# Chunked mLSTM state kept as row pairs of 64-row tiles instead of three-head blocks

## The chip, the cores and the metric

The kernel runs on one core of one Trainium2 chip. The metric is the device time of one execution in microseconds (us); the median of three runs stands for the kernel. One more execution was recorded by the hardware profiler, and all rows below come from it.

A core has five engines that work in parallel, each on its own queue in order: PE (TensorE, matrix products; its weight loads are listed apart as PEld), DVE (VectorE), ACT (ScalarE), POOL (GpSimd) and SP (SyncE, which here issues the DMAs). They wait for each other through semaphores. PE writes to PSUM, eight banks of 128 partitions by 512 float32 numbers; the other data lie in SBUF.

## The reference

Three layers follow one another. The change is in the first, a gated linear attention (mLSTM), over batch B = 2, heads H = 8, sequence S = 768, head size D = 40:

```python
for t in range(S):
    m_new = np.maximum(f_gate[:, :, t] + m, i_gate[:, :, t])
    f_stab = np.exp(f_gate[:, :, t] + m - m_new)
    i_stab = np.exp(i_gate[:, :, t] - m_new)
    m = m_new
    C = f_stab[:, :, None, None] * C + i_stab[:, :, None, None] * np.einsum('bhd,bhe->bhde', vt, kt)
    n = f_stab[:, :, None] * n + i_stab[:, :, None] * kt
    h_tilde = np.einsum('bhde,bhe->bhd', C, qt)
    nq = np.einsum('bhd,bhd->bh', n, qt)[:, :, None]
    y[:, :, t] = sigmoid(o_gate) * h_tilde / np.maximum(np.abs(nq), 1.0)
```

Behind it come a gated MLP with a mixing product along the sequence (`w_in`, `w_sp`, `w_out`) and a channel mix with squared ReLU (`w_k`, `w_v`, `w_r`). They are not touched.

## The kernel before

The sequence is cut into six chunks of 128 tokens; with two batches that makes twelve work items i, taken in the order `SEQ` (L44): chunk 0 of both batches, then chunk 1 of both, and so on. The item i - 1, on whose state item i rests, is therefore two positions earlier. Within a chunk the recurrence becomes matrix products:

- `scores` (L444) multiplies queries and keys of the chunk (tiles sc), `logd` (L474) makes the decay between two tokens (ld, then dt), `intra` (L570) multiplies the weighted scores with the values (av). The queries and keys of heads 0 to 3 lie on partitions 0 to 39, those of heads 4 to 7 on 64 to 103, so a product of 40 rows takes the upper or the lower half of PE's array; the matmuls of heads g and 4 + g alternate and write to two banks.
- `state` (L514) multiplies the keys, weighted by POOL in `key_weights` (kw, L503), with the values: what the chunk adds to the state (sp). Three heads stand together (`GRP`, L56): a product of 128 tokens by 120 rows by 123 columns holds nine 40 by 41 blocks, of which the three on the diagonal are wanted. ACT fades the old state with three activations (`fade`, L533, from `dec`), and DVE takes the wanted blocks out of PSUM with three operations under a block mask (`gather`, L541). The state is cn.
- `inter` (L552) reads the state with a second copy of the queries, laid out by groups of three heads, that comes with the keys and values in one load (kvq, `load_kv`, L331): three matmuls per item (ip), and one DVE operation that scales the result by a gate (nn).
- `normalise` (L583) adds both parts, `turn` (L615) transposes the result (tp, then xg).

In float32 each of these matmuls stands in the trace as two pairs of a weight load and a matmul record.

The order on each engine is made by a planner while the program is built. A position p of the pipeline holds tasks (`task`, L894): S0 (scores of the next item), I (`inter`), T (`state`), N0 and N1 (the two halves of `intra`), X (`turn`). The planner keeps its own clock with costs written in the code (`beat`, `chain`), takes the first of four tasks whose inputs it thinks ready, and fills in between with matmuls of the MLP's input product (`vpart`, `upart`: tiles vp and up), so many per task as `FILL` (L890) says. Where none is ready it issues junk matmuls (`heat`, tile wp). The elementwise work of a task is a chain of steps on DVE, ACT and POOL. PSUM tiles of this part come from a ring of six banks (`bank`, tag "at"): a matmul that starts a new tile waits until the tile six banks earlier has been read.

While this runs, weights of 64-bit words are turned into pairs of float32r tiles by `widen` (L252), in steps on ACT, DVE and POOL (tiles wbits, wsq, and w_v, w_u at the end).

The lines that the change touches are these:

Of the kernel before, what the change touches and what calls it, by code (L numbers as in the profile page):

```python
# [17 lines left out]
def tile_mlstm_gmlp_channelmix(  # L18
# [26 lines left out]
    P = 128  # L45
# [10 lines left out]
    GRP = ((0, 3), (3, 3), (6, 2))  # L56
# [239 lines left out]
    def rows3(t, w):  # L296
# [10 lines left out]
                            for nm, n in (("f2", P), ("i2", P), ("ex_sb", 120), ("pk_sb", 6 * NCH)))  # L307
    bm_sb = at.tile([120, 3], F32, name="bm_sb")
    mg = gp.tile([16, S + 1], F32, name="mg")
    ones = gp.tile([96, P], F32, name="ones")  # L310
    dec = at.tile([120, 6, NCH], F32, name="dec")
# [11 lines left out]
    def load_qk(i):  # L323
        b, c = divmod(i, NCH)
        t = at.tile([P, 2, 4, P], F32, tag="qk", name=f"qk{i}", bufs=2)
        for hh in range(2):
            e = load(t[64 * hh:64 * hh + D], qk[b, c, hh], 164)
        st["q", i], st["k", i] = t[:, 0], t[:, 1]
        st["at", i] = e

    def load_kv(i):  # L331
        b, c = divmod(i, NCH)
        n = H * D + H * DA + (3 * P if c > 0 else 0)
        t = at.tile([P, H * D + H * DA + 3 * P], F32, tag="kvq", name=f"kvq{i}", bufs=2)
# [3 lines left out]
        if c > 0:  # L338
            st["qc", i] = t[:120, H * (D + DA):].rearrange("p (g t) -> p g t", g=3)
# [174 lines left out]
    def state(i):  # L514
        b, c = divmod(i, NCH)
        vt = st["vt", i]
        if c == NCH - 1:
            return
        wait(("kw", i))
        kw = st.pop(("kw", i))  # L520
        sp = bank(psa, "at", f"sp{i}", ("Cs", i))
        if c == 0:
            st["C", b] = at.tile([120, H * DA], F32, name=f"cn{b}")
        cn = st["C", b]
# [6 lines left out]
        s3, c3 = (t.rearrange("p (h d) -> p h d", h=H) for t in (sp[:, :H * DA], cn))  # L531

        def fade():  # L533
            if i == SEQ[0]:
                act.copy(bm_sb, bm_raw)
            if c > 0:
                for g, (h0, n) in enumerate(GRP):
                    sl = slice(h0 * DA, (h0 + n) * DA)
# [7 lines left out]
        if c == 0:  # L546
            pool.memset(cn, 0.0)
        else:
            finish(("dec", 0), stall=False)
        chain(("C", i), ("A", 0.75 if c else 0.2, fade), ("V", 1.0, gather, ("Cs", i)))  # L550

    def inter(i):  # L552
        b, c = divmod(i, NCH)
        if c == 0:
            return
        wait(("C", i - 1))
        qt, cs = st.pop(("qc", i)), st["C", b]
        ip = bank(psa, "at", f"ip{i}", ("nn", i))
        for g, (h0, n) in enumerate(GRP):
# [5 lines left out]
        chain(("nn", i), ("V", 0.41, lambda: vec.tensor_tensor(  # L565
            out=nn, in0=ip[:, :H * DA].rearrange("p (h d) -> p h d", h=H), op=ALU.mult,
            in1=egate(b, c, 0).unsqueeze(2).to_broadcast([P, H, DA]))))
# [272 lines left out]
    bm_raw = at.tile([120, 3], F32, name="bm_raw")  # L840
    m2 = gp.tile([96, 2, P], F32, name="m2")
    lpk = gp.tile([96, 6 * NCH], F32, name="lpk")
# [8 lines left out]
    for a in 'k0 v0 q6 k6 v1 b v2 n'.split():  # L851
        dict(k=lambda: load_kv(SEQ[a != "k0"]), q=lambda: load_qk(SEQ[1]), n=lambda: load_qk(SEQ[2]),
             v=lambda: w_in_load("v", 1, int(a[1])), b=lambda: load(bm_raw, blockmask[:, 0:3 * DA:DA], 2))[a[0]]()
    w_in_split("v", hv)
    chain(("G0", 1), ("V", 0.26, lambda: scan(1, 2)), *[("V", 0.28, f) for f in late_steps], ready=6.9)
# [21 lines left out]
    for t, x in ((ex_sb, expand), (pk_sb, pick)):  # L877
        load(t, x, 48)
# [4 lines left out]
    def decays():  # L883
        dps = bank(psa, "at", "dps", ("dec", 0))
        pe.matmul(dps[:120, :6 * NCH], ex_sb, lpk, start=True, stop=True)
        beat(0.15)
        chain(("dec", 0), ("A", 0.1, lambda: act.activation(out=dec.rearrange("p j c -> p (j c)"),
                                                            in_=dps[:120, :6 * NCH], func=AF.Exp)))

    FILL = (6, 4, 1, 3, 1, 1, 1, 4)  # L890
# [6 lines left out]
    def position(p):  # L897
# [22 lines left out]
        def st_():  # L920
# [5 lines left out]
            state(i)  # L926
# [413 lines left out]
```

## Time and profile before

| | before |
|---|---|
| median of 3 runs | 307.42 us (307.24 to 307.59) |
| profiled execution | 307.6 us, span 305.9 us from the first to the last instruction |
| attention with its fillers | from about 8 us to 129 us of the span |
| PE busy / PEld busy | 296.7 us (97%) / 281.0 us (92%) |
| DVE / ACT / POOL busy | 225.0 us / 165.7 us / 143.7 us |
| granted TensorE clock | 1.000 of full speed (2.4 GHz) |

The busy time of PE overlaps itself, since matmuls are pipelined and their ends are modelled: how fast PE goes is read from the distance between starts, or from the pieces of the chain of waits, which do not overlap.

### The profile page before, as it was taken

The numbers are of one execution on the slowest core, as the hardware profiler recorded it, in microseconds if no ns is written. First come the engines' busy times: TensorE is split into PE (matmuls) and PEld (weight loads), VectorE is DVE, ScalarE is ACT, GpSimd is POOL, SyncE is SP. The second block draws the span as 40 slices with busy tenths as digits, with TensorE's granted clock in tenths as the row PEclk, the third lists the DMA queues.
The fourth block names the chain that finished last, engine by engine and source line by source line (L and its number), as shares of the span: only waits on it lengthen the run. The fifth ranks groups of instructions, "written<-read, shape, count | busy, mean of one in ns | idle before, by whom it ended". The sixth has DMA issues, their size and how long they took to land.

```text
span 305.9 us, 5522 instructions
## 1 busy us (share of the span) xinstructions
PE 296.7 (97%) x2014; PEld 281.0 (92%) x2014; DVE 225.0 (74%) x449; ACT 165.7 (54%) x348; POOL 143.7 (47%) x171
## 2 busy tenths in 40 slices
PE   8999988799999999999999999999999999999995
PEld 6887867698988998999999999999999999999995
DVE  7799899765858667765798989978966755745611
ACT  3644779544655435553354473586966745734610
POOL 5155353834758843763474636563625304303500
PEclk9999999999999999999999999999999999999999
DMA  5969672443343301157033412231010010001001
GB/s 148 288 183 282 207 270 79 141 137 121 95 142 83 104 24 30 58 168 245 3 86 108 143 43 73 65 122 44 2 43 25 0 43 24 0 27 40 0 24 43
DMA packets 13937, 28.74 MB, mean 94 GB/s; under 512 B 2407, under 2 KB 7783, under 8 KB 13911
## 3 DMA queue, kind: packets, MB, share of 16 engines
q1 hardware_dynamic: 13879, 28.33, 30.2%
q8 instruction: 16, 0.26, 0.4%
q0 software_dynamic: 32, 0.07, 0.1%
q14 instruction: 10, 0.08, 0.1%
HBM read 26.20 MB, written 1.97 MB: 92 GB/s over the span
## 4 chain that ended last, share of the span: by engine, by line
PE 83%; DVE 6%; ACT 4%; issue 2%; DMA 1%; POOL 1%; SPq 1%; DVEq 0%; ACTq 0%
PE spp L653 16%; PE kp L653 15%; PE vv L653 14%; PE up L653 8%; PE wop L653 7%; PE vp L653 6%; PE rp L653 5%; PE av L580 5%; PE sc L456 3%; DMA og<-in_o_tok_dram 1%; PE ip L560 1%; PE sp L526 1%; PE ld L488 1%; PE tp L628 1%; ACT og L348 1%
## 5 line engine op out<-in xcount | busy, mean ns | idle before, releaser
L1183 POOL TENSOR_TENSOR sq<-sq 128x384 f32<-128x384 f32 x32 | 29.5, 929 | 46.4 <-ACT sq L1182 46.3
L653 PE MATMUL spp<-wsp,vn 128*128 128x384 f32 x288 | 50.4, 334 | 0.0
L653 PEld LDWEIGHTS spp<-wsp,vn 128*128 128x128 f32 x288 | 49.9, 188 | 0.0
L653 PE MATMUL kp<-xk,wk 128*128 128x384 f32 x256 | 45.3, 334 | 0.0
L653 PEld LDWEIGHTS kp<-xk,wk 128*128 128x128 f32 x256 | 44.5, 188 | 0.0
L653 PE MATMUL vv<-wv,k 128*128 128x320 f32 x288 | 43.2, 309 | 0.0
L653 PEld LDWEIGHTS vv<-wv,k 128*128 128x128 f32 x288 | 42.4, 188 | 0.3 <-POOL wv L234 0.3
L234 DVE TENSOR_TENSOR k<-sq,k 128x384 fp32r<-128x384 f32 x32 | 26.1, 818 | 13.6 <-ACT k L1184 13.6
L653 PE MATMUL up<-xg,w_u 128*128 128x256 f32 x192 | 30.3, 293 | 1.4 <-POOL w_u L234 1.4
L653 PE MATMUL vp<-w_v,xg 128*128 128x512 f32 x96 | 28.8, 415 | 1.3 <-DVE xg L234 1.3
L1080 POOL TENSOR_TENSOR vs<-vs,u 128x384 f32<-128x384 f32 x16 | 19.6, 1228 | 21.1 <-DVE vs L1079 21.1
L653 PEld LDWEIGHTS up<-xg,w_u 128*128 128x128 f32 x192 | 25.6, 191 | 2.2 <-POOL w_u L234 1.6
L278 DVE SCALAR_TENSOR_TENSOR wbits<-wsq,wbits 128x320 int32<-128x320 int32 (+1 forms) x27 | 23.3, 865 | 3.7 <-ACT wsq L273 3.1
L580 PE MATMUL av<-kvq,dt 128*128 128x123 f32 (+1 forms) x192 | 24.5, 272 | 0.0
L580 PEld LDWEIGHTS av<-kvq,dt 128*128 128x128 f32 x192 | 23.9, 191 | 0.6
L1182 ACT ACTIVATE sq<-kp 128x384 f32<-128x384 f32 x32 | 15.6, 490 | 14.9 <-PE kp L653 12.9
L653 PE MATMUL wop<-gt,wo 128*128 128x384 f32 x128 | 22.8, 334 | 0.0
L653 PEld LDWEIGHTS wop<-gt,wo 128*128 128x128 f32 x128 | 22.2, 188 | 0.0
L653 PEld LDWEIGHTS vp<-w_v,xg 128*128 128x128 f32 x96 | 17.1, 189 | 4.6 <-DVE xg L234 2.2
L234 POOL TENSOR_TENSOR vn<-vr,vn 128x512 fp32r<-128x512 f32 x12 | 15.9, 1323 | 9.1 <-ACT vn L731 9.1
L1223 DVE TENSOR_TENSOR ob<-rs,vv 128x320 f32<-128x320 f32 x12 | 5.8, 486 | 18.6 <-PE vv L653 17.5
L282 DVE SCALAR_TENSOR_TENSOR wsq<-wraw,wbits 128x320 int32<-128x320 int32 (+1 forms) x21 | 17.9, 854 | 0.3
(183 smaller groups left out, 563.3 us busy)
## 6 DMA issues: line engine op xcount, KB each, us to landing
kvq<-in_kvq_dram SPq DMA_DIRECT2D x10, 516.0 KB
qk<-in_qk_dram SPq DMA_DIRECT2D x24, 160.0 KB
wraw<-in_w_k_dram SPq DMA_DIRECT2D x6, 512.0 KB
wraw<-in_w_v_dram SPq DMA_DIRECT2D x8, 320.0 KB
wraw<-in_w_sp_dram SPq DMA_DIRECT2D x12, 192.0 KB
og<-in_o_tok_dram SPq DMA_DIRECT2D x12, 160.0 KB
out_dram<-ob SPq DMA_DIRECT2D x12, 160.0 KB
w_inv<-in_w_in_dram SPq DMA_DIRECT2D x3, 512.0 KB
```

What stands on the lines that cost most here:

```text
L234: eng.tensor_tensor(out=out, in0=a, in1=b.bitcast(F32), op=ALU.subtract)
L278: vec.scalar_tensor_tensor(out=t["bits"], in0=t["sq"].bitcast(I32), scalar=3, in1=t["bits"], op0=ALU.logical_shift_left, op1=ALU.bitwise_or)
L282: vec.scalar_tensor_tensor(out=t["sq"].bitcast(I32), in0=t["high"], scalar=SIGN, in1=t["bits"], op0=ALU.bitwise_and, op1=ALU.bitwise_or)
L348: act.activation(out=st["o", b, c], in_=st["o", b, c], func=AF.Sigmoid)
L456: pe.matmul(st["sc", i, x][:, h * P:(h + 1) * P], k_[64 * x:64 * x + D, h, :], q_[64 * x:64 * x + D, h, :], start=True, stop=True)
L488: pe.matmul(ld, lts[c % 2][:, b], rl[:, hh * 512:(hh + 1) * 512], start=True, stop=not early)
L580: pe.matmul(av[:, own_, :], A[:, h, :], vt[:, own_, :], start=True, stop=True)
L653: pe.matmul(out[0], l, x, start=j == 0, stop=j == len(prs) - 1)
L1080: ("P", 1.29, lambda: pool.tensor_tensor(out=vs, in0=vs, in1=ut[b][:, d, sl], op=ALU.mult)),
L1182: chain(("k2", g, f), ("A", 0.49, lambda: act.activation(out=sq, in_=ps, func=AF.Relu), ("kp", g, f)), ("P", 0.96, lambda: pool.tensor_ten ...
L1183: ("P", 0.96, lambda: pool.tensor_tensor(out=sq, in0=sq, in1=sq, op=ALU.mult)),
L1223: vec.tensor_tensor(out=ob, in0=rs, in1=ps, op=ALU.mult)
```

## The change

Heads g and 4 + g now stand in one row pair of the state: cn is a tile of 128 partitions by 4 by 41, head g on partitions 0 to 39 and head 4 + g on 64 to 103, as the queries of `scores` do. `state` makes eight small products per item, 128 tokens by 64 or 40 rows by 41 columns, one for each head, written to partitions 0 and 64 of a bank (the 64 takes 24 rows of the next head along, which are never read). `inter` reads the state with the queries that `scores` used, in eight products of 40 rows by 128 tokens by 41 columns, that alternate between both halves and two banks. The two tasks I and T become one: sp is written into the free half of the first ip bank right behind ip. The fade is one POOL operation, the gather one DVE addition, and for chunk 0 one ACT copy. nn is scaled in two halves. The second copy of the queries is no longer loaded (kvq loses 384 of 1032 columns), the query tiles get a third buffer because they are read later, and the constants `ex_sb` and `pk_sb` are added up from the identity by DVE; the loads of `expand`, `pick` and `blockmask` go.

```diff
-    GRP = ((0, 3), (3, 3), (6, 2))
...
-        t = at.tile([P, 2, 4, P], F32, tag="qk", name=f"qk{i}", bufs=2)
+        t = at.tile([P, 2, 4, P], F32, tag="qk", name=f"qk{i}", bufs=3)
...
-        n = H * D + H * DA + (3 * P if c > 0 else 0)
+        n = H * D + H * DA
...
     def state(i):
...
-        for g, (h0, n) in enumerate(GRP):
-            pe.matmul(sp[:n * D, h0 * DA:(h0 + n) * DA],
-                      kw[:, h0:h0 + n, :].rearrange("p h d -> p (h d)"),
-                      vt[:, h0:h0 + n, :].rearrange("p h d -> p (h d)"), start=True, stop=True)
-        beat(0.57)
...
-                    act.activation(out=cn[:n * D, sl], in_=cn[:n * D, sl], func=AF.Copy, scale=dec[:n * D, 3 * b + g, c:c + 1])
-
-        def gather():
-            for j, r in enumerate((D, 2 * D, 3 * D)):
-                vec.scalar_tensor_tensor(out=c3[:r, j:H:3], in0=s3[:r, j:H:3], in1=c3[:r, j:H:3],
-                                         scalar=bm_sb[:r, j:j + 1], op0=ALU.mult, op1=ALU.add)
...
+        for g in range(4):
+            for x in range(2):
+                h, m = 4 * x + g, D if x else 64
+                pe.matmul(sp[64 * x:64 * x + m, g * DA:(g + 1) * DA], kw[:, h * D:h * D + m], vt[:, h, :], start=True, stop=True)
+        beat(0.7)
+        s4 = sp[:64 + D, :4 * DA].rearrange("p (g d) -> p g d", g=4)
+        if c == 0:
+            chain(("C", i), ("A", 0.3, lambda: act.copy(cn[:64 + D], s4), ("Cs", i)))
             return
...
+        finish(("dec", 0), stall=False)
+        chain(("C", i),
+              ("P", 0.5, lambda: pool.tensor_tensor(out=cn[:64 + D], in0=cn[:64 + D], op=ALU.mult,
+                                                    in1=dec[:64 + D, b, :, c:c + 1].to_broadcast([64 + D, 4, DA]))),
+              ("V", 0.3, lambda: vec.tensor_tensor(out=cn[:64 + D], in0=cn[:64 + D], in1=s4, op=ALU.add), ("Cs", i)))
 
     def inter(i):
...
-        for g, (h0, n) in enumerate(GRP):
-            pe.matmul(ip[:, h0 * DA:(h0 + n) * DA], qt[:n * D, g, :], cs[:n * D, h0 * DA:(h0 + n) * DA],
-                      start=True, stop=True)
...
+        ip = [bank(psa, "at", f"ip{i}_{x}", ("nn", i), *[("Cs", i)] * (x == 0 and c < NCH - 1)) for x in range(2)]
+        for g in range(4):
+            for x in range(2):
+                r = slice(64 * x, 64 * x + D)
+                pe.matmul(ip[x][:, (4 + g) * DA:(5 + g) * DA], q_[r, g, :], cs[r, g, :], start=True, stop=True)
         nn = at.tile([P, H, DA], F32, tag="nn", name=f"nn{i}", bufs=2)
-        beat(0.57)
+        beat(0.5)
+        if c < NCH - 1:
+            st["ipsp", i] = ip[0]
+            state(i)
...
+        chain(("nn", i), ("V", 0.25, gate(0)), ("V", 0.25, gate(1)))
...
-    FILL = (6, 4, 1, 3, 1, 1, 1, 4)
+    FILL = (6, 5, 1, 3, 1, 1, 1, 4)
```

On PE, at position 7 (the ip at 74.29 us and the sp at 75.44 us of the trace), this stood between two stretches of filler matmuls; ip is the read of the state, sp the new state, up the filler, and the last figures are output partitions by columns:

```order
L653 MATMUL up_0_1061<-xg_569,w_u_624 128x256
L560 MATMUL ip_1069<-cn_372,kvq_917 128x123 x2
L560 MATMUL ip_1069<-cn_372,kvq_917 128x82
L653 MATMUL up_0_1061<-xg_569,w_u_623 128x256 x2
L653 MATMUL up_0_1061<-xg_569,w_u_624 128x256
L653 MATMUL up_1_1080<-xg_569,w_u_623 128x256
L526 MATMUL sp_1083<-kvq_917,kw_1024 120x123 x2
L526 MATMUL sp_1083<-kvq_917,kw_1024 80x82
L653 MATMUL up_1_1080<-xg_569,w_u_624 128x256
```

After the change the same place reads so; between the first and last rows of each kind lie six more that alternate in the same way:

```order
L644 MATMUL up_0_1075<-xg_559,w_u_610 128x256
L544 MATMUL ip_0_1083<-cn_349,qk_809 128x41
L544 MATMUL ip_1_1084<-cn_349,qk_809 128x41
...
L524 MATMUL ip_0_1083<-kvq_913,kw_1038 64x41
L524 MATMUL ip_0_1083<-kvq_913,kw_1038 40x41
...
L644 MATMUL up_0_1075<-xg_559,w_u_609 128x256 x2
L644 MATMUL up_0_1075<-xg_559,w_u_610 128x256
```

Six matmuls became sixteen, and the fillers that stood between the two groups now stand behind both.

On DVE, at position 3, the gather stood between the statistics of an MLP tile (sb) and the subtraction (xg) for which PE's next fillers wait:

```order
L709 BN_STATS sb_661<-vr_660 128x6
L565 TENSOR_TENSOR nn_666<-ip_662,egb 128x328
L712 BN_AGGR sb_661<-sb_661 128x2
L713 TENSOR_SCALAR sb_661<-sb_661 128x1
L543 SCALAR_TENSOR_TENSOR cn_372<-sp_670,bm_sb,cn_372 40x3x41
L543 SCALAR_TENSOR_TENSOR cn_372<-sp_670,bm_sb,cn_372 80x3x41
L543 SCALAR_TENSOR_TENSOR cn_372<-sp_670,bm_sb,cn_372 120x2x41
L725 SCALAR_TENSOR_TENSOR sb_661<-sb_661 128x1
L234 TENSOR_TENSOR xg_434<-tp_687,xg_434 128x2x128
```

After the change it reads:

```order
L700 BN_STATS sb_644<-vr_643 128x6
L534 TENSOR_TENSOR cn_349<-cn_349,ip_0_649 104x164
L703 BN_AGGR sb_644<-sb_644 128x2
L704 TENSOR_SCALAR sb_644<-sb_644 128x1
L554 TENSOR_TENSOR nn_659<-ip_0_649,egb 128x164
L554 TENSOR_TENSOR nn_659<-ip_1_650,egb 128x164
L233 TENSOR_TENSOR xg_417<-tp_679,xg_417 128x2x128
```

Three operations of the gather became one addition, nn became two, and the small step on sb (L716) moved behind xg.

## Rows read from the trace of the kernel before

**Rows 1.** The page: the span, and the chain that ended last by engine.

```profile
span 305.9 us, 5522 instructions
...
PE 83%; DVE 6%; ACT 4%; issue 2%; DMA 1%; POOL 1%; SPq 1%; DVEq 0%; ACTq 0%
```

**Rows 2.** Busy time by stretch: us, each engine (records), granted clock, DMA share, GB/s.

```profile
18.00:27.00 9.00, 8.59 (x70) 6.84 (x70) 8.73 (x23) 4.82 (x10) 5.22 (x6) 1.00 0.72 207
27.00:41.00 14.00, 13.92 (x115) 12.03 (x114) 13.03 (x33) 7.71 (x18) 6.05 (x8) 1.00 0.81 265
41.00:62.00 21.00, 17.01 (x130) 13.87 (x129) 18.19 (x46) 17.38 (x37) 12.02 (x15) 1.00 0.42 125
62.00:100.00 38.00, 38.00 (x319) 34.52 (x319) 26.36 (x74) 20.59 (x48) 23.01 (x33) 1.00 0.41 123
100.00:129.00 29.00, 28.98 (x209) 27.04 (x208) 19.99 (x49) 13.14 (x30) 16.82 (x22) 1.00 0.16 48
```

**Rows 3.** PE's timeline: start, us, work, and in brackets the idle time before.

```profile
26.67 0.96 PE L653 MATMUL vp<-w_v,xg 128*128 128x512 f32 x3 [0.41 <-DVE xg L234]
...
44.81 0.96 PE L653 MATMUL vp<-w_v,xg 128*128 128x512 f32 x3 [0.89 <-DVE xg L234]
...
51.06 0.50 PE L488 MATMUL ld<-rl,lt 128*128 128x512 f32 x1 [0.35 <-ACT dt L498]
...
53.99 1.13 PE L456 MATMUL sc<-qk 40*128 40x128 f32 x14 [0.96 <-issue]
...
60.13 0.38 PE L653 MATMUL up<-xg,w_u 128*128 128x256 f32 x1 [1.36 <-POOL w_u L234]
```

**Rows 4.** The chain of waits, 71.9 to 79 us: start, us, what.

```profile
71.94 1.09 PE sc L456 x16
73.03 0.43 PE ld L488
...
74.29 0.63 PE ip L560 x6
...
75.44 0.57 PE sp L526 x6
...
76.17 0.89 PE av L580 x8
...
77.86 0.23 PE ld L488
...
78.21 0.82 PE av L580 x8
```

**Rows 5.** The chain of waits, 18 to 61 us.

```profile
18.90 0.54 PE wp L356 x4
...
20.07 1.10 PE wp L356 x7
...
21.39 0.67 DVE cn L543 x3
...
33.28 0.80 DVE cn L543 x3
...
41.83 0.85 ACT cn L539 x3
...
53.09 0.80 DVE cn L543 x3
...
58.84 1.25 POOL w_u L234
```

**Rows 6.** Groups of instructions by line and shape, 0 to 130 us: count, busy us, mean ns.

```profile
L595 POOL TENSOR_TENSOR og<-og,nn 128x320 f32<-128x320 f32 x12 | 10.2, 851 | 3.1 <-DVE nn L599 3.1
...
L600 ACT COPY nn<-av 128x328 f32<-128x328 f32 x2 | 0.9, 430 | 0.3 <-PE av L580 0.3
...
L565 DVE TENSOR_TENSOR nn<-ip,egc 128x328 f32<-128x328 f32 x8 | 3.9, 492 | 1.9 <-PE ip L560 1.8
...
L401 DVE TENSOR_TENSOR i<-i,m 96x128 f32<-96x128 f32 x1 | 0.3, 275 | 0.0
```

More of the change, by code (lines that the diff above doesn't have):

```diff
@@ L306, in tile_mlstm_gmlp_channelmix @@
     f2, i2, ex_sb, pk_sb = (gp.tile([96, n], F32, name=nm)
-                            for nm, n in (("f2", P), ("i2", P), ("ex_sb", 120), ("pk_sb", 6 * NCH)))
-    bm_sb = at.tile([120, 3], F32, name="bm_sb")
+                            for nm, n in (("f2", P), ("i2", P), ("ex_sb", 2), ("pk_sb", B * 4 * NCH)))
     mg = gp.tile([16, S + 1], F32, name="mg")
     ones = gp.tile([96, P], F32, name="ones")
-    dec = at.tile([120, 6, NCH], F32, name="dec")
+    dec = at.tile([P, B, 4, NCH], F32, name="dec")
     jk = gp.tile([P, 2 * P], BF16, name="jk")
@@ L546, in state @@
[L546 to L550, printed above, removed]
+        wait(("kw", i))
+        kw = st.pop(("kw", i)).rearrange("p h d -> p (h d)")
+        sp = st.pop(("ipsp", i), None)
+        if sp is None:
+            sp = bank(psa, "at", f"sp{i}", ("Cs", i))
+            st["C", b] = at.tile([P, 4, DA], F32, name=f"cn{b}")
+        cn = st["C", b]
@@ L849, in late_rows @@
             st["late"] = load(m2[:, w], mg[:, w:w + S], 48, 14.0)
-    for a in 'k0 v0 q6 k6 v1 b v2 n'.split():
+    for a in 'k0 v0 q6 k6 v1 v2 n'.split():
         dict(k=lambda: load_kv(SEQ[a != "k0"]), q=lambda: load_qk(SEQ[1]), n=lambda: load_qk(SEQ[2]),
-             v=lambda: w_in_load("v", 1, int(a[1])), b=lambda: load(bm_raw, blockmask[:, 0:3 * DA:DA], 2))[a[0]]()
+             v=lambda: w_in_load("v", 1, int(a[1])))[a[0]]()
     w_in_split("v", hv)
+    rest4 = id_sb[:96, :96].rearrange("p (b x r) -> p b x r", b=B, x=2)
+    late_steps += [lambda: vec.tensor_reduce(out=ex_sb, in_=rest4.rearrange("p b x r -> p x b r"), axis=mybir.AxisListType.XY,
+                                             op=ALU.add),
+                   lambda: vec.tensor_tensor(out=pk_sb.rearrange("p (b r) -> p b r", b=B), in0=rest4[:, :, 0], in1=rest4[:, :, 1],
+                                             op=ALU.add)]
     chain(("G0", 1), ("V", 0.26, lambda: scan(1, 2)), *[("V", 0.28, f) for f in late_steps], ready=6.9)
@@ L884, in decays @@
         dps = bank(psa, "at", "dps", ("dec", 0))
-        pe.matmul(dps[:120, :6 * NCH], ex_sb, lpk, start=True, stop=True)
+        for x in range(2):
+            pe.matmul(dps[64 * x:64 * x + 64, :B * 4 * NCH], ex_sb[:, x:x + 1].to_broadcast([96, 64]), lpk, start=True, stop=True)
         beat(0.15)
-        chain(("dec", 0), ("A", 0.1, lambda: act.activation(out=dec.rearrange("p j c -> p (j c)"),
-                                                            in_=dps[:120, :6 * NCH], func=AF.Exp)))
-    FILL = (6, 4, 1, 3, 1, 1, 1, 4)
+        chain(("dec", 0), ("A", 0.1, lambda: act.activation(out=dec.rearrange("p b g c -> p (b g c)"),
+                                                            in_=dps[:, :B * 4 * NCH], func=AF.Exp)))
+    FILL = (6, 5, 1, 3, 1, 1, 1, 4)
     HOT = (0, 1, 0, 0, 3, 2, 0)
@@ L925, in st_ @@
                 vec.tensor_scalar(out=omu_sb, in0=mu_sb, scalar1=-1.0, scalar2=1.0, op0=ALU.mult, op1=ALU.add)
-            state(i)
+            if i % NCH:
+                inter(i)
+            else:
+                state(i)
         def tr():
@@ L1017, in tile_mlstm_gmlp_channelmix @@
         best["fn"]()
[L1018 to L1019 removed]
+        lsp = lsp_[0] if lsp_ else None
         passed.add(best["name"])
```

46 lines of the change are left out of this document (11 added, 35 removed).

## The prediction, made before the changed kernel had run

> **What bounds the kernel now.** I read the page first. Its chain that ended last is PE for 83% of the span [rows 1], so added PE work is paid wherever PE has no slack. The busy time by stretch says where that is [rows 2]: from 62 to 129 us PE is busy for practically all of 67 us, while DVE, ACT and POOL are not (26.36, 20.59 and 23.01 us of 38). From 41 to 62 us PE is busy for only 17.01 of 21 us, and DVE and ACT are nearly full (18.19 and 17.38). From 18 to 41 us PE and DVE are both full, but PE's time holds junk matmuls, two pieces of 0.54 and 1.10 us [rows 5]. Then PE's timeline for its waits [rows 3]: 0.41, 0.89, 0.35, 0.96 and 1.36 us, 3.97 us together, all before 61 us; none names a DMA. The 0.96 us has no releaser named, but the gather that starts at 53.09 and takes 0.80 us [rows 5] ends 0.1 us before the matmul at 53.99: it had held the PSUM bank of sp. So the kernel has two regimes. Up to 60 us the chain runs through DVE, ACT and POOL, and the old fade and gather stand in it four times [rows 5]. Behind 60 us it is PE alone, to the end.
>
> **How fast PE goes.** The pieces of the chain give it [rows 4]. The first half of `intra` (av at 76.17, 0.89 us) makes eight loads of 128 weight columns and streams 984 columns; the second (78.21, 0.82 us) makes the same eight loads and streams 738. A quarter fewer streamed columns, 8% less time: the loads set the pace, 0.80 to 0.87 ns per weight column. ip agrees (6 loads, 768 weight columns, 0.63 us: 0.82 ns), and sp nearly (640 weight columns, 0.57 us: 0.89 ns). I take 0.83 ns.
>
> The only products on parts of the array are sc: 16 records on 40 rows, alternating halves, 128 weight columns each. At 0.83 ns the eight loads of one half take 0.85 us; if both halves load side by side that is the whole block. It takes 1.09 us, and the ld behind it 0.43 us where the same ld elsewhere takes 0.23 [rows 4]: 1.29 us in all. Two things follow: the halves do load side by side (one after the other would be 1.70 us), and going into the halved array and out again costs 1.29 - 0.85 = 0.44 us, 0.22 us each way.
>
> **PE's part of the change.** Each float32 matmul is two load and matmul records (ip has six for three matmuls [rows 4]).
> - ip becomes 16 records on the two row halves with 128 weight columns each, as sc has: 0.85 us, though it streams 41 columns instead of 123.
> - sp becomes 16 records with 64 and 40 weight columns in turn, on the two column halves. No row shows column halves. Side by side: 8 x 64 x 0.83 = 0.43 us; one after the other: 8 x 104 x 0.83 = 0.69 us. I take the middle, 0.56, since nothing leans to either side.
> - Whole array to row halves, row halves to column halves, column halves to whole: three switches of 0.22 us, 0.66 us.
>
> Together 0.85 + 0.56 + 0.66 = 2.07 us per item, against 0.63 + 0.57 = 1.20 before: +0.87 us. This is the step on which the forecast stands. The two last items read a state and make none: 0.85 + 0.44 - 0.63 = +0.66 us each. The two first make one and read none: 0.56 + 0.44 - 0.57 = +0.43 us each.
>
> The Trainium skill, page "TensorEngine Tiling", section "Key Properties", states that a change of the tiling mode, other than a change of tile, drains the engine. The 0.44 us around sc are this trace's number for it. Without the drains the merged task would take 1.41 us by the rows and the total would hardly move; that speaks against this change, because it adds three such changes of mode per item where there were none.
>
> Behind 60 us lie four items with both, of which [rows 4] show the second, and two with ip alone: 4 x 0.87 + 2 x 0.66 = **+4.8 us**, all on the path. Cover there is none: PE is busy for 38.00 of 38.00 us [rows 2]. Their bounds: if tiles were paced by what they stream, a pair costs 0.106 x 41/128 = 0.034 us, ip and sp 0.27 us each, the merged task 1.20 and ip alone 0.71, in all +0.2 us; with the column halves one after the other, +5.3 us.
>
> **The other engines' part, up to 60 us.** From the chain go [rows 5]: a gather of 0.67 us for chunk 0 (ACT copies instead, between 0.22 and 0.43 us by its copy of twice the size [rows 6], beside DVE; ACT is busy 4.82 of 9 us there, and where that cover fails it costs its own time), gathers of 0.80 and 0.80 us, and a fade of 0.85 us: 3.12 us. Into it come:
> - the two sums that make ex_sb and pk_sb on DVE. The nearest row is 0.275 us for 128 columns [rows 6]; these read 96, so between zero and that each: 0.55 us;
> - a DVE addition of 164 columns at 33 and 53 us: between half and all of the 0.492 us for 328 columns from PSUM [rows 6], I take 0.33 each, 0.66 us;
> - nn in two halves, by the same number 2 x 0.3 instead of 0.49, twice: 0.2 us;
> - a fade on POOL, 164 of 320 columns at 0.851 us [rows 6], 0.44 us. Queued behind it stands the third subtraction for w_u (1.25 us at 58.84 [rows 5]), for which PE waits 1.36 us.
>
> Net -3.12 + 1.85 = -1.3 us. PE's own work up to there: 2 x 0.43 + 4 x 0.87 = +4.3 us, less the junk (1.64 us) and less all waits (3.97 us): -1.3 us if no wait were left. Both sides come to the same, and since they alternate I take **-1.2 us**, between -1.3 and +0.2 (half of the waits stay and POOL is late by one more fade).
>
> **At nothing** I put the loads. Ten kvq loads are shorter and three small loads go, but no wait of PE ends in a DMA [rows 3], and DMA is 1% of the chain [rows 1]; a third query buffer lets loads start earlier, for which nobody waits. The DVE and ACT time saved behind 62 us is not on the path. The wait for kw moves ahead of ip, but POOL has 15 of 38 us to spare there [rows 2]. If kw were late, both halves of the task would stand, and with them all of PE.
>
> **Sum.** -1.2 + 4.8 = +3.6 us. The profiled execution took 307.6 us, 0.2 us over the median of 307.42; on the median the forecast is **311.0 us**, slower by 1.2%.
>
> **Rivals.**
> 1. *Small tiles are paced by the columns they stream* (faster). sc cannot refute it: its 128 streamed columns would take what its 128 weight columns take. Against it: the two halves of av, on the whole array. PE then gains nothing and loses nothing, and the chain of DVE, ACT and POOL decides: -1.3 + 0.2 gives 306.3 us. It decides once the merged task takes under 1.4 us: with ip alone in proportion, each microsecond over 1.20 counts 4 + 2 x 0.66/0.87 = 5.5 times, and 1.2/5.5 = 0.22. The Trainium skill, page "TensorE: Matmul & The Clock Gate", section "Part 3: Packing small matmuls", gives the span of a packed group as one matmul's time and some 4 ns per further tile, which is this case; its figures are for 512 columns.
> 2. *The switches overlap with loads* when two tiled groups follow each other directly: 1.41 us per item, +0.21, ip alone +0.22: 4 x 0.21 + 2 x 0.22 - 1.2 gives 307.5 us, no change.
> 3. *POOL becomes late.* It gets eight fades of 0.44 us, and in 41 to 62 us it releases PE's longest wait. If four of them stand in that way, 4 x 0.44 = 1.8 us come on top: 312.8 us. Against it: it is busy for 12.02 of 21 us.
> 4. *The clock falls.* The merged task streams little for some 2 us. The granted clock is 1.00 in all stretches, also where PE stood for 1.36 us [rows 2, 3], so I hold it unlikely. If a tenth of the 38 us from 62 to 100 us ran at 1.2 GHz instead of 2.4, up to 3.8 us would come on top: 314.8 us.
>
> **How the numbers follow.** Forecast 0.65, rival 1 0.15, rival 2 0.09, rival 3 0.07, rival 4 0.04. A change under 0.2% (0.6 us) can't be told from none here. Faster: rival 1 and a little of the forecast's low end, 0.16. Same: rival 2 and 0.01, 0.10. Slower: the rest, 0.74. The forecast's own range is 308.5 (sp side by side, cheaper switches) to 313.0 us (+5.3 and +0.2). To leave out no more than 2 in 10 of all cases it must reach down past rival 1, to 305.9, and up past rival 3, to 314.0.
>
> **What would show it.** Right: in the chain behind 62 us an ip of 0.85 us or more and an sp of 0.43 to 0.69 us, with 0.2 us of extra distance where each begins and behind sp; a PE without waits from 62 to 129 us; less waiting before 60 us. Wrong: an ip under 0.6 us or pieces without the extra distance (rivals 1, 2), a PE wait on POOL longer than 1.36 us (rival 3), a granted clock under 1.00 (rival 4), or waits before 60 us that have not shrunk, so that the loss is larger.

## The result, and the profile after

| | before | changed |
|---|---|---|
| median of 4 runs each | 307.33 us (306.85 to 307.59) | 310.74 us (310.42 to 311.18) |
| ratio, 95% interval | | 1.0114 [1.0093, 1.0134] |
| profiled execution, span | 307.6, 305.9 us | 310.42, 308.7 us |
| granted TensorE clock of the profiled execution | 1.000 | 0.994 |

The change made the kernel 3.4 us slower; the forecast was 311.0 us. From one profile to the other it is 2.8 us: the profiled execution of before lies 0.3 us over its median, that of the changed kernel 0.3 us under. Some executions of several kernels below, though none of the four of the changed kernel, ran 3 to 8 us longer with a mean granted clock of 0.97 to 0.99; those over 1.5% above a kernel's fastest are left out of its ratio, and where medians still hold some, the clock is given beside the time.

The busy time of the changed kernel, with the columns of [rows 2]: by the same stretches, and below that by microsecond at one place:

```profile
18.00:27.00 9.00, 7.41 (x55) 5.54 (x54) 8.63 (x17) 4.60 (x12) 6.03 (x6) 1.00 0.91 266
27.00:41.00 14.00, 13.76 (x149) 11.53 (x149) 10.98 (x32) 6.28 (x14) 5.26 (x8) 1.00 0.52 181
41.00:62.00 21.00, 19.83 (x186) 16.79 (x186) 17.66 (x44) 14.70 (x27) 13.58 (x18) 0.92 0.33 98
62.00:100.00 38.00, 38.00 (x381) 33.72 (x379) 22.13 (x63) 16.71 (x34) 21.80 (x34) 1.00 0.30 91
100.00:129.00 29.00, 29.00 (x218) 26.30 (x215) 19.82 (x53) 12.45 (x27) 17.02 (x23) 1.00 0.18 55
...
55.00:56.00 1.00, 0.98 (x22) 0.81 (x20) 1.00 (x3) 0.81 (x1) 0.82 (x2) 1.00 0.50 126
56.00:57.00 1.00, 0.41 (x2) 0.44 (x3) 0.86 (x4) 0.98 (x2) 0.29 (x1) 0.59 0.29 94
57.00:58.00 1.00, 1.00 (x7) 1.00 (x6) 1.00 (x1) 0.64 (x2) 0.98 (x1) 0.50 0.56 133
...
59.00:60.00 1.00, 1.00 (x7) 0.96 (x6) 0.75 (x2) 0.58 (x2) 1.00 (x3) 0.71 0.00 0
```

Against [rows 2], DVE and ACT are lighter in the third and fourth stretch (ACT 14.70 for 17.38, DVE 22.13 for 26.36 us), PE fills 19.83 of 21 us where it filled 17.01, and behind 62 us it is still full. New is a granted clock of 0.92 from 41 to 62 us.

PE's timeline of the changed kernel, all its waits from 18 to 62 us:

```profile
19.62 1.13 PE L452 MATMUL sc<-qk 40*128 40x128 f32 x14 [0.32 <-DMA qk<-in_qk_dram]
25.20 1.81 PE L644 MATMUL vp<-w_v,xg 128*128 128x512 f32 x5 [1.17 <-ACT xg L633]
34.40 0.50 PE L644 MATMUL vp<-w_v,xg 128*128 128x512 f32 x1 [0.24 <-ACT xg L633]
50.81 0.50 PE L484 MATMUL ld<-rl,lt 128*128 128x512 f32 x1 [0.27 <-ACT dt L494]
53.64 0.47 PE L484 MATMUL ld<-rl,lt 128*128 128x512 f32 x1 [0.18 <-issue]
56.59 2.04 PE L571 MATMUL av<-kvq,dt 128*128 128x123 f32 x8 [0.61 <-DVE dn L593]
```

The waits of [rows 3] for DVE's xg, for POOL's w_u and for the bank of sp (0.96 us) are gone. What is left sums to 2.79 us. Before it was 4.33 us: the 3.97 us of the prediction and two short waits that it left out:

```profile
41.82 0.50 PE L488 MATMUL ld<-rl,lt 128*128 128x512 f32 x1 [0.17 <-DVE dt L501]
55.30 0.47 PE L488 MATMUL ld<-rl,lt 128*128 128x512 f32 x1 [0.19 <-issue]
```

The longest that is left is new: 1.17 us for xg, whose cast on ACT stands behind a cast (of w_v) for which ACT itself waited 1.44 us for DVE.

The chain of waits of the changed kernel, behind the av at 56.59 us, and for the item of [rows 4]:

```profile
58.63 0.71 PE tp L619 x3
59.35 0.21 PE up L644
59.56 0.30 PE ld L484
...
71.73 1.09 PE sc L452 x16
72.83 0.43 PE ld L484
73.25 0.23 PE vp L644
73.49 0.60 PE up L644 x5
74.08 1.02 PE ip L544 x16
75.10 0.59 PE ip L524 x13
75.69 0.79 PE up L644 x5
76.49 0.89 PE av L571 x8
...
77.74 0.33 PE tp L619 x3
78.06 0.12 PE up L644
78.19 0.23 PE ld L484
```

L544 is ip, L524 is sp (it writes into ip's tile now). From sc to av it takes 76.49 - 71.73 = 4.76 us where [rows 4] take 76.17 - 71.94 = 4.23 us, with the same fillers between (one vp, ten up): **+0.53 us** for the merged task. The task itself is 1.02 + 0.59 us and 0.19 us by which the five up behind it are longer than the five ahead of it: 1.80 us, against the predicted 2.07.

The sums over the program follow from starts. The sc at 71.73 us is 0.21 us earlier than in [rows 4]; one merged task lies between it and 62 us, so at 62 us the change was ahead by **0.74 us**. The twelfth sc starts at 99.06 us (97.69 before, +1.37), three merged tasks later: 1.58 us, 0.53 each. The first spp starts at 132.08 us (129.22 before, +2.86): 1.49 us for the two items with ip alone. Together: -0.74 + 4 x 0.53 + 1.49 = +2.9 us at the first spp. From there to the end the two kernels take the same time within 0.1 us.

The clock falls to 1.2 GHz in the wait of 0.61 us that follows sc, ld, ip and sp (0.59 in the microsecond from 56 us), and is back within the one from 59 us (0.71): about 3.4 us. The av in it takes 2.04 us, and the chain's first three pieces 0.71, 0.21 and 0.30 us; its last three are the same work at 2.4 GHz, 0.33, 0.12 and 0.23 us. In other executions the clock fell at other points near this one, as the experiments show.

The small operations, as groups by line and shape:

```profile
L532 POOL TENSOR_TENSOR cn<-cn,dec 104x164 f32<-104x164 f32 x8 | 4.0, 504 | 2.7 <-PE ip L544 2.7
L534 DVE TENSOR_TENSOR cn<-cn,ip 104x164 f32<-104x164 f32 x8 | 2.5, 313 | 0.0
L554 DVE TENSOR_TENSOR nn<-ip,egc 128x164 f32<-128x164 f32 x16 | 4.7, 320 | 2.4 <-PE ip L524 1.3 <-PE ip L544 1.1
L528 ACT COPY cn<-sp 104x164 f32<-104x164 f32 x2 | 0.6, 293 | 0.4 <-PE sp L524 0.4
L848 DVE TENSOR_REDUCE ex_sb<-id_sb 96x2 f32<-96x96 f32 x1 | 0.2, 232 | 0.0
```

### The profile page after: what moved, and what is told of

Same layout as the page of the kernel before. It is cut to its first block, busy times and chain, and to the rows that moved or that the text cites. A ratio compares the mean times of both kernels' runs of the same rounds, so it can differ in the third digit from the quotient of the medians.

```text
span 308.7 us, 5862 instructions
## 1 busy us (share of the span) xinstructions
PE 300.6 (97%) x2205; PEld 283.4 (92%) x2205; DVE 219.2 (71%) x439; ACT 159.1 (52%) x325; POOL 146.4 (47%) x177
## 4 chain that ended last, share of the span: by engine, by line
PE 84%; DMA 5%; ACT 3%; issue 2%; DVE 2%; SPq 1%; POOL 1%; POOLq 0%; DVEq 0%; ACTq 0%
PE spp L644 16%; PE kp L644 14%; PE vv L644 14%; PE up L644 8%; PE wop L644 7%; PE vp L644 6%; PE av L571 5%; PE rp L644 5%; DMA qk<-in_qk_dram 3%; PE sc L452 2%; PE ip L544 2%; DMA kvq<-in_kvq_dram 2%; PE ld L484 1%; PE tp L619 1%; PE ip L524 1%
## 5 line engine op out<-in xcount | busy, mean ns | idle before, releaser
L1076 POOL TENSOR_TENSOR vs<-vs,u 128x384 f32<-128x384 f32 x16 | 19.6, 1229 | 20.8 <-DVE vs L1075 19.4
L644 PE MATMUL up<-xg,w_u 128*128 128x256 f32 x192 | 29.0, 291 | 0.0
L571 PE MATMUL av<-kvq,dt 128*128 128x123 f32 (+1 forms) x192 | 25.8, 279 | 0.6 <-DVE dn L593 0.6
L571 PEld LDWEIGHTS av<-kvq,dt 128*128 128x128 f32 x192 | 24.9, 197 | 1.5 <-PE ip L524 0.7
L277 DVE SCALAR_TENSOR_TENSOR wbits<-wsq,wbits 128x320 int32<-128x320 int32 (+1 forms) x27 | 20.9, 774 | 4.1 <-ACT wsq L272 3.7
```

Source lines behind the costliest of these rows:

```text
L277: vec.scalar_tensor_tensor(out=t["bits"], in0=t["sq"].bitcast(I32), scalar=3, in1=t["bits"], op0=ALU.logical_shift_left, op1=ALU.bitwise_or)
L571: pe.matmul(av[:, own_, :], A[:, h, :], vt[:, own_, :], start=True, stop=True)
L644: pe.matmul(out[0], l, x, start=j == 0, stop=j == len(prs) - 1)
L1076: ("P", 1.29, lambda: pool.tensor_tensor(out=vs, in0=vs, in1=ut[b][:, d, sl], op=ALU.mult)),
```

## The experiments

All but two are edits of the changed kernel. The theory was that of the prediction: PE pays for ip and sp in halves behind 60 us, and what DVE, ACT and POOL gain counts only before. The rivals were that another engine or the clock had made the difference.

**ip twice** (the price of the row halves without a switch):

```diff
-        for g in range(4):
+        for g in (0, 1, 2, 3) * (2 if SEQ.index(i) >= 6 else 1):
             for x in range(2):
                 r = slice(64 * x, 64 * x + D)
```

> The changed kernel with ip's sixteen records issued twice in direct succession in the six items whose ip lies behind 62 us; the second set writes the same numbers over the first. Nothing else moves. It gives the price of the row halves without a switch. Theory (loads set the pace: eight pairs of 128 weight columns at 0.80 to 0.83 ns each): 0.82 to 0.85 us more per item, 4.9 to 5.1 us in all, 315.6 to 315.8 us. Rival 1 of the prediction (the 41 streamed columns set the pace): 0.27 us per item, 1.6 us in all, 312.4 us.

Its chain of waits at the ninth item:

```profile
76.51 1.91 PE ip L544 x32
78.42 0.59 PE ip L524 x13
```

1.91 - 1.02 = 0.89 us for eight pairs of 128 weight columns, 0.87 ns each. The time was 317.15 us (315.96 to 317.84), ratio 1.0327 [1.029, 1.0364], more than the six repeats can make (5.4 us): in its profile every engine's order up to 62 us is that of the changed kernel, yet the eighth sc starts 1.53 us later there, because the clock stayed at 1.2 GHz until 62.8 us (a clock of 0.50 in each microsecond from 56 to 62 us, 0.60 in the next) instead of 59.6. From the eighth sc to the first spp it loses 5.4 us, six times 0.89 and a little more than the theory's 4.9 to 5.1 us; the rival's 1.6 us is out.

**sp twice** (the column halves without a switch): the same edit in the loop of `state`.

> The changed kernel with sp's sixteen records issued twice in direct succession in the four items whose sp lies behind 62 us; the second set writes the same numbers over the first. Nothing else moves. It gives the price of the column halves without a switch. Theory now (halves load side by side: eight loads of 64 weight columns, with the 40 of the other half beside them): 0.43 to 0.47 us more per item, 1.7 to 1.9 us in all, 312.4 to 312.6 us. The other bound of the prediction (one half after the other, 104 columns): 0.69 us per item, 2.8 us in all, 313.5 us.

The chain of waits at the same item:

```profile
74.78 1.02 PE ip L544 x16
75.80 1.06 PE ip L524 x25
```

1.06 - 0.59 = 0.47 us: the halves load side by side, eight loads of 64 columns at 0.91 ns. The time was 313.07 us (312.49 to 313.53), 1.0200 [1.0178, 1.0221], 2.3 us more than the changed kernel, between the two forecasts; the trace decides, where the first spp starts 2.12 us later than in the changed kernel, 1.9 us of it in the four items.

**ip and sp directly behind sc** (two switches fewer per item; the fillers that stood between the tasks stand behind the joined one):

```diff
             scores(n, 0)
+            if joined:
+                st_()
             logd(n, 0)
...
-            task(("T", i), st_, [("kw", i)] * (c < NCH - 1) + [("C", i - 1)] * (c > 0), [("N1", prev)] + ["G"] * (p >= 2),
-                 slot=1 if c else 2, p=p)
+            if not joined:
+                task(("T", i), st_, tkeys, [("N1", prev)] + ["G"] * (p >= 2), slot=1 if c else 2, p=p)
```

> The changed kernel with ip and sp issued directly behind the scores sc of the next item (eight items, five of them behind 60 us), ahead of ld, where it stood behind ld and some fillers. sc and ip use the same row halves, so an item loses two switches of the array: out of sc and into ip. Nothing that is computed changes. Theory of the prediction (a switch is paid at about 0.2 us each): 0.40 to 0.44 us less per item, 2.0 to 2.2 us less behind 60 us and up to 1.3 us before; 307.5 to 309.0 us. Rival (the switches overlap with loads, and ip and sp are simply longer): no change within 0.4 us, 310.7 us. A third possibility is that ld, now 1.6 us later, makes the exponentials late: then new waits of PE on ACT or DVE appear before av and the time rises.

Measured: 313.56 us (312.84 to 314.03), 1.0209 [1.0191, 1.0228]. The pieces of its chain show that the switches went:

```profile
71.72 1.09 PE sc L452 x16
72.81 0.82 PE ip L544 x16
73.63 0.59 PE ip L524 x13
74.22 0.43 PE ld L484
```

ip costs 0.82 us instead of 1.02, and from sc to av it takes 0.16 us less than in the changed kernel (4.60 us): less than half of what the theory gave. New waits of PE ate it and more. What PE waited for from 40 to 130 us (us in total, times, longest):

```profile
PE ld L484 <- DMA rl<-Lxc: 3.4, 3, 1.6
PE up L644 <- ACT u L735: 1.4, 1, 1.4
```

The second ld of an item reads the tile rl, into which the load issued behind the first ld writes; ip and sp had stood between them as cover. So it was the third possibility, with a DMA in the place of ACT and DVE. In the profiled execution the clock also fell, from 89.3 to 92.8 us, 1.5 us behind the wait for rl that ended at 87.86 us, while PE was busy:

```profile
89.38 2.20 PE vp L644 x5
91.59 1.66 PE sc L452 x16
```

The same pieces take 1.23 and 1.09 us in the changed kernel: 1.5 us more. The other three runs, at clocks of 0.998 to 1.000, took 312.84 to 313.60 us, so the loss against the changed kernel is not that of the clock.

**The same, with that load moved** (an edit of the kernel just told):

```diff
-            if p % 2 == 0 and 2 <= p < NT - 2:
+            if p % 2 == 0 and 2 == p < NT - 2:
                 gate_rows(p // 2 + 1)
...
             logd(n, 1)
+            if p % 2 == 0 and 4 <= p < NT - 2:
+                gate_rows(p // 2 + 1)
```

> The run in which ip and sp follow the scores directly, with the load of the next gate rows moved from behind the first ld to behind the second ld of the item (from the fifth position on). In the run before, the second ld waited 0.91, 0.97 and 1.56 us for that load, which writes into rl, the tile that the second ld reads: ip and sp no longer stood between them as cover. What is computed is the same. Theory (those waits were all that the joining cost, and each joined item saves some 0.3 us of switches, by the pieces of that run's trace: sc 1.09 to 1.00, ip 1.02 to 0.92, the up ahead of ip 0.1): the time falls from 313.6 by 2.5 to 3.4 us, to 310.2 to 311.1 us, and without the other new wait (1.39 us for ACT's u) to 309.0 us or so. Rival (the joining makes ld and the exponentials late whatever the load does): waits of PE on ACT, DVE or POOL ahead of av take the place, and the time stays above 312 us.

Measured: 312.87 us (five runs, 310.87 to 313.09, at clocks of 0.984 to 0.994), 1.0165 [1.0137, 1.0193]. The waits for rl are gone, but PE now waits 2.28 us for ACT's u at 103.7 us and 0.71 us for DVE ahead of an ip, and the clock fell twice in the profiled execution, for some 3.4 us each. The theory's 310.2 to 311.1 us was missed by four of the five runs, and waits of the kind that the rival named are there: a saving of 0.16 us per item is no match for one of them. What the joining alone is worth in time stays open.

**The relief given back** as dummies on ACT and DVE (chain steps of 0.75 and 1.3 us in the planner's costs; three ACT and three DVE operations per item):

```diff
-        chain(("C", i),
+        chain(("C", i), ("A", 0.75, old_fade),
...
-              ("V", 0.3, lambda: vec.tensor_tensor(out=cn[:64 + D], in0=cn[:64 + D], in1=s4, op=ALU.add), ("Cs", i)))
+              ("V", 1.3, old_gather, ("Cs", i)))
```

> The changed kernel with the removed work of DVE and ACT given back as dummies in the same place of the chain of states: per item three ACT copies with a scale (123, 123 and 82 columns, ahead of POOL's fade) and three DVE scalar_tensor_tensor operations of two or three blocks with the addition, all into scratch or, for the addition, as now. The output's state is the same as without the dummies; they are additional work only. Theory: the relief of DVE and ACT counts up to 60 us and not behind it. Then the time rises by what the prediction put as removed from the chain (3.1 us at most, 1 to 3 us here, to 312 to 314 us), all of it lost before 62 us, and the stretch from 62 us to the end is as long as in the changed kernel within 0.3 us. Rival (PE and its clock alone decide, the relief was worth nothing): within 0.5 us of 310.7 us.

Measured: 311.36 and 311.75 us in the two runs whose clock was that of the changed kernel or better (0.998, 0.994), the profile among them, where spp starts 0.94 us later; the other four, at clocks of 0.968 to 0.984, took 314.42 to 319.14 us, and the ratio of those kept is 1.0196 [1.0156, 1.0237]. The waits of PE that returned, in its timeline:

```profile
53.70 1.16 PE L454 MATMUL sc<-qk 40*128 40x128 f32 x14 [1.01 <-ACT dt L496]
61.52 0.33 PE L633 MATMUL tp<-id_sb,x 128*128 128x128 f32 x1 [1.05 <-POOL x L613]
```

Both lie before 62 us, and from 62 to 129 us PE is busy for 66.84 of 67 us. So the place is the theory's. The size, 0.6 to 1.0 us in two runs, lies between the rival's 0.5 us and the 1 to 3 us of the theory, and in the profiled execution the clock did not fall from 56 us as it did in the changed kernel's, so it is a rough number.

**The fade back on ACT** in the changed kernel:

```diff
-              ("P", 0.5, lambda: pool.tensor_tensor(out=cn[:64 + D], in0=cn[:64 + D], op=ALU.mult,
-                                                    in1=dec[:64 + D, b, :, c:c + 1].to_broadcast([64 + D, 4, DA]))),
+              ("A", 0.8, lambda: [act.activation(out=cn[:64 + D, g], in_=cn[:64 + D, g], func=AF.Copy,
+                                                 scale=dec[:64 + D, b, g, c:c + 1]) for g in range(4)] and None),
```

> The changed kernel with one part undone: the state is faded by ACT again (four multiplications of 41 columns on 104 rows, in the place of GpSimd's one). What is computed is the same. Theory (from the run of the kernel before with GpSimd's fade, 1.9 us shorter, all of it ahead of 62 us: the fade's move is the valuable part of the change, and the new ip and sp cost more than it gives): 1 to 2.5 us slower than the changed kernel, 311.7 to 313.2 us, all of it ahead of 62 us. Rival (in the changed kernel DVE and ACT had been relieved anyway by the shorter gathers, so that ACT has room for 0.8 us per item): within 0.5 us of 310.7 us.

Measured: 314.20 us (312.91 to 314.31), 1.0208 [1.0182, 1.0234]: 3.5 us slower than the changed kernel, more than expected. In PE's timeline a wait of 1.31 us is new:

```profile
54.35 2.04 PE L452 MATMUL sc<-qk 40*128 40x128 f32 x14 [1.31 <-issue]
```

The busy time by stretch around it shows the clock:

```profile
53.00:55.00 2.00, 0.69 (x7) 0.68 (x8) 1.95 (x7) 1.78 (x4) 1.41 (x2) 0.83 0.64 156
55.00:58.00 3.00, 3.00 (x23) 2.34 (x21) 2.59 (x8) 1.47 (x3) 2.20 (x3) 0.50 0.29 83
58.00:62.00 4.00, 4.00 (x35) 3.84 (x34) 1.61 (x5) 1.36 (x5) 3.32 (x4) 0.50 0.26 84
```

Behind the wait PE stands at 1.2 GHz, for all of 55 to 62 us and some 2 us of the next stretch (0.97 in 62 to 100 us). That is some 10 us at 1.2 GHz, where the changed kernel had 3.4 us. Up to the seventh sc this kernel is only 0.25 us behind the changed one, at the eighth 4.42 us: most of the loss lies where the clock is low, and what ACT's own work costs without it was not separated.

**The fade on GpSimd alone**, in the kernel before:

```diff
-                for g, (h0, n) in enumerate(GRP):
-                    sl = slice(h0 * DA, (h0 + n) * DA)
-                    act.activation(out=cn[:n * D, sl], in_=cn[:n * D, sl], func=AF.Copy, scale=dec[:n * D, 3 * b + g, c:c + 1])
+                for n, g in ((120, slice(0, 2)), (80, slice(2, 3))):
...
+                    pool.tensor_tensor(out=cn[:n, r].rearrange("p (g d) -> p g d", d=w), op=ALU.mult,
...
-        chain(("C", i), ("A", 0.75 if c else 0.2, fade)
+        chain(("C", i), ("P" if c else "A", 0.9 if c else 0.2, fade)
```

> The kernel before with one part of the change alone: the three ACT operations that fade the old state (0.85 us in the chain) are done by two GpSimd multiplications, of 246 columns on 120 rows and 82 columns on 80 rows; matmuls, gathers and loads stay those of before. What is computed is the same. Theory of the prediction's early part (the chain of DVE and ACT up to 60 us gives back what is taken from it, ACT was busy 8.75 of 9 us from 41 to 50 us): GpSimd takes about 0.65 + 0.25 us, so the chain itself gains nothing, ACT gains 0.85 us per item: 0 to 0.8 us faster, 306.3 to 307.1 us against 307.1 of before. Rival (POOL becomes late: the third subtraction for w_u stands behind the fade and PE waits for it): 0.5 to 1.8 us slower, 307.6 to 308.9 us.

Measured: 305.52 us, median of twelve, against 307.25 us of before; 0.997 [0.9937, 1.0003]. Eight of the twelve had a clock of 0.998 or more and took 304.75 to 305.70 us; the other four, at 0.981 to 0.989, took 307.1 to 309.1 us and make the interval as wide as it is. In the profile (305.41 us) spp starts at 127.35 us, 1.87 us earlier than before, and all of it is there at the ninth sc (70.07 us for 71.94). All twelve are faster than the changed kernel. Against the kernel before there is a gain at a clock of 0.998 or more, larger than I expected: its five executions at that clock on the same chip took 306.12 to 307.25 us. Over all twelve no gain on it is shown, since the interval reaches 1: the executions with a lower clock took 2 us and more longer.

**And chunk 0 copied by ACT** besides, in that kernel:

```diff
+        def pick0():
+            for j, r in enumerate((D, 2 * D, 3 * D)):
+                act.activation(out=c3[:r, j:H:3], in_=s3[:r, j:H:3], func=AF.Copy, scale=bm_sb[:r, j:j + 1])
+
+        if c == 0:
+            chain(("C", i), ("A", 0.2, fade), ("A", 0.7, pick0, ("Cs", i)))
+            return
```

> The kernel before with two parts of the relief and none of the new matmuls: GpSimd fades the state, as in the run of that alone, and for the first chunk three ACT copies with the mask as scale take the place of the three DVE gathers (0.67 us) into the cleared state. What is computed is the same. Theory: DVE is full from 18 to 41 us and ACT is not (4.8 of 9 us busy from 18 to 27), so one more gather twice off DVE gives 0.2 to 0.7 us over the fade alone: 304.7 to 305.2 us where that took 305.4 us. Rival: from 18 to 27 us the weights' splitting on DVE and POOL sets the pace, which the gather doesn't delay, or ACT's copies stand ahead of its weights' casts: no change within 0.2 us, or 0.3 to 1 us slower than the fade alone. Either way it stays under the 307.3 us of before.

Measured: 307.40 us, 1.0014 [0.9977, 1.0051]; the six runs at a clock of 0.998 or more took 305.82 to 306.17 us. Their median, 306.1 us, is 1.0 us more than that of the fade alone at such a clock (305.1): the rival. Taking work off a DVE that is full was no gain here; which of the rival's two reasons held was not looked into.

**The constants loaded** instead of made on DVE:

```diff
-    late_steps += [lambda: vec.tensor_reduce(out=ex_sb, in_=rest4.rearrange("p b x r -> p x b r"), axis=mybir.AxisListType.XY,
...
+    for t, x in ((ex_sb, expand), (pk_sb, pick)):
+        load(t, x, 48)
```

> The changed kernel with the two constants ex_sb and pk_sb loaded by DMA again (in the new shapes) instead of being summed on DVE. The constants themselves are the same. Theory: the two sums cost what the prediction gave them, at most 0.55 us on DVE ahead of the first items, and part of it shows: 0 to 0.5 us faster, 310.2 to 310.7 us. Rival: the two small loads stand in the way of the first large ones in the queue, whose landing paces the first 18 us; then 0.3 to 1 us slower, and the part made on chip was a gain of the change.

Measured: 310.40 to 311.54 us in the four runs at 0.994 and 0.998, ratio 1.0129 [1.0111, 1.0147], which overlaps that of the changed kernel. No difference can be told.

**Junk against the fall of the clock**, twice:

```diff
+            if p == 5:
+                now = clock[0]
+                heat(6)
+                clock[0] = now
```

The first version put the six junk matmuls behind the same task without `now`, and the planner moved eight up ahead.

> The changed kernel with six junk matmuls put behind ip and sp of the item whose task ends at 55.8 us, where the granted clock then fell to 0.50 for about 3.4 us. What is computed is the same. Theory A: the fall of the clock is paid in full, since PE's work in it (av 2.04 us for about 0.85, three tp 0.71 for 0.33) stands on the path. With the junk the clock stays at 1.00 there and the time falls by 1.2 to 1.6 us, to about 309.3 us. Theory B: the clock's fall is covered, since w_u's third subtraction on POOL, which ends at 60.9 us, releases PE anyway; then the time stays within 0.3 us of 310.7 whatever the clock does. If the clock falls all the same, the run tells nothing about its price.

> The changed kernel with six junk matmuls behind ip and sp of the same item as in the first junk run, but with the planner's clock set back, so that every other instruction of every engine stands in the order of the changed kernel (the first junk run also moved eight matmuls of up ahead, which then waited 2.07 us for POOL's w_u). What is computed is the same. Theory A: the 3.4 us at half clock are paid; the junk fits into PE's wait of 0.61 us for DVE at 56.6 us, the clock stays at 1.00, and the time falls by 1.2 to 1.9 us from 310.7, to 308.8 to 309.5 us. Theory B: the next thing PE needs (dt, x, POOL's w_u) comes no earlier, so PE waits instead of running slowly: within 0.4 us of 310.7 us, with new waits of PE between 57 and 62 us that add up to 1.2 us or more. If the clock falls all the same, the run tells nothing.

The first took 311.58 us (three runs, all at a clock of 1.000), 1.0148 [1.013, 1.0166]. The clock held, and PE ran into POOL, as its timeline shows:

```profile
56.55 0.83 PE L352 MATMUL wp<-id_sb 128*128 128x256 bf16 x6
...
61.17 0.39 PE L644 MATMUL up<-xg,w_u 128*128 128x256 f32 x1 [2.07 <-POOL w_u L233]
```

The second took 310.82 us (four runs), 1.0110 [1.0085, 1.0136], no change. Two of the four had a clock of 0.999 and 1.000 (310.33 and 310.97 us), two one of 0.993 and 0.994 (310.67 and 311.05 us). In its profiled execution (317.74 us, clock 0.972) the clock fell all the same, in the middle of sp and ahead of the junk, with PE busy since 60.98 us:

```profile
62.67 0.95 PE L524 MATMUL ip<-kvq,kw 128*64 128x41 f32 x16
63.55 1.46 PE L352 MATMUL wp<-id_sb 128*128 128x256 bf16 x6
...
62.00:63.00 1.00, 1.00 (x24) 0.95 (x22) 1.00 (x4) 0.48 (x1) 1.00 (x2) 0.92 0.41 102
```

So the waits that take the place of a low clock are not shown, nor that it was the junk that kept the clock up where it held. Theory A's price of 1.2 us or more is out.

## Why the prediction was right

**The regimes** were read rightly: behind 62 us every added microsecond of PE was paid, before it the other engines' relief counted. The two halves of the sum were each off, in opposite directions: +4.8 was +3.6 us, -1.2 was -0.74 us. By the profiles that makes +2.9 us where the forecast had +3.6; that the medians came within 0.3 us of it, because both profiled executions lie off their medians, is luck.

**The pace of halves.** Predicted: weight columns set it, 0.83 ns each. Shown by ip twice (0.87 ns) and sp twice (0.91 ns). ip takes 0.89 us for the predicted 0.85; sp is near the lower bound of 0.43, 0.47 us for the 0.56 in the middle that I took. Rival 1 is refuted: ip streams 41 columns where sc streams 128, at nearly the same pace (1.02 and 1.09 us for sixteen records). The Trainium skill, page "TensorE: Matmul & The Clock Gate", section "Part 3: Packing small matmuls", gives the span of a packed group as one matmul's time and some 4 ns per further tile. Rival 1 had read that for this shape, and it does not hold here: ip's second set of sixteen records, which share two halves of the array, took 0.89 us, 56 ns per record.

**The switches** were the mis-sized term: 3 x 0.22 = 0.66 us. Measured: 1.02 - 0.89 = 0.13 us into the row halves, 0.59 - 0.47 = 0.12 us from row to column halves, 0.19 us out, 0.44 us. I had read 0.44 us off sc and its ld, half for each way; the joined kernel, which saves one way out and one way in, gained 0.16 us in the same row. They do cost something, 0.12 to 0.19 us each, so rival 2 is refuted. The Trainium skill, page "TensorEngine Tiling (Array Packing)", section "Key Properties", says that a change of mode drains the engine; the trace, with these distances, agrees.

**The old form** was under-counted. ip and sp each broke the fillers once: the up behind them take 0.52 + 0.16 us in the chain of before where five in a row take 0.59, 0.08 us that the merged task saves. Together: 2.07 + 0.04 - 0.09 - 0.22 = 1.80 us, less 1.28, is +0.52 us per item where I had +0.87. ip alone cost 0.75 us each, by the starts of the last sc and of spp, for the predicted 0.66.

**Up to 60 us.** The prices held (POOL's fade 0.504 us for 0.44, DVE's addition 0.313 for 0.33, half of nn 0.320 for 0.3, ACT's copy 0.293, ex_sb's sum 0.232 for 0.275). The waits shrank by 1.5 us only. One that I did not foresee came up, 1.17 us for xg on ACT at 25 us: another order came out of the planner, with the casts of w_v and Lxc ahead of xg, where xg had come first. How much of it is paid was not tried. The value of the relief depends on which part it is: dummies for all of it cost 0.6 to 1.0 us, the fade alone brought 1.9 us in the kernel before at a clock of 1.00 and cost 3.5 us when it went back to ACT in the changed one, most of it in a stretch of low clock. So the fade's move is the one part of the change for which a gain was seen, and the new ip and sp, at +3.6 us, cost more than that.

**Rival 3**, POOL late, did not come: no wait of PE names POOL. The first junk run shows that it was near, 2.07 us once eight up were moved ahead. **Rival 4**, the clock, did come, at a place where I had not looked for it: I argued from [rows 2, 3] that PE may stand for 1.36 us at a clock of 1.00. That was one execution: of the 51 executions of the kernel before that ran beside the experiments, 29 had a mean clock of 0.988 to 0.994, so the clock falls in that kernel too. The 21 of them at 0.992 to 0.994 had a median of 307.2 us, the 22 at 0.998 or more one of 307.1 us: there such a fall cost nothing that can be told. The merged task was not shown to be what makes it fall. How much of the changed kernel's 3.4 us at 1.2 GHz is paid is not settled to better than this: the pieces behind its av are 0.54 us longer than at 2.4 GHz, in the second junk run the two executions without a fall were 0.2 us faster on average, and in sp twice PE waits 0.25 us for DVE's x behind an av of 1.64 us, so part of av's delay is covered. A longer fall is paid: ip twice lost 1.5 us with it. So is one behind 62 us: 1.5 us of longer pieces in the joined kernel.

**At nothing.** Behind 62 us no wait names a DMA or kw, as predicted. One of 0.32 us for qk at 19.6 us is new, and the chain of the changed kernel runs through that load from 10.30 to 19.48 us, so the loads were not quite at nothing; the part of it that is paid was not tried.

## What to carry to other kernels

A product that is cut into parts of PE's array and streams few columns (here 41 for 64 or 128 weight columns) pays by the weight columns it loads, not by what it streams, and every change between whole array, row halves and column halves costs 0.1 to 0.2 us here: products of one mode belong side by side, unless other work then loses its cover. Where one stretch is bound by PE and another by the elementwise engines, a change that trades between them should be taken apart: here the fade's move to GpSimd alone, without the new products, beat the changed kernel, and at the full clock the kernel before as well. And one profiled execution with a clock of 1.00 does not say that the clock holds in the others: the mean granted clock belongs beside every time that is compared.

## What the runs showed of the hardware

- Two row halves of 128 weight columns load side by side at 0.87 ns per column, two column halves of 64 and 40 at 0.91 ns per column of the wider.
- Around the same merged task the granted clock fell to half at different points: 0.2 us into PE's wait of 0.61 us in the changed kernel, 0.1 us ahead of that wait with ip twice, 0.4 us behind it with sp twice, and 0.2 us into sp, without a wait, in the profiled execution of the second junk run. In the profiled execution of the kernel before it did not fall in a wait of 1.36 us that followed other work [rows 3]; in the first junk run, with six junk matmuls behind sp and then a wait of 2.07 us, it stayed at 1.00.
- The same order of instructions had falls of different length: to 59.6 us in the changed kernel, to 62.8 us in the run with ip twice, 1.5 us apart at the next sc.
- GpSimd multiplied 164 columns on 104 rows in 0.504 us.
